# Transposing the attention's exponentials directly in front of P's first part, and splitting the attention one and a half slots sooner

## The chip, the cores and the metric

The kernel runs on one core of one Trainium2 chip. The metric is the device time of one execution in microseconds (us), the median of the runs of one version. Engines are called as the profile calls them: PE (matrix multiplication) with PEld (its weight loads), DVE (vector), ACT (scalar, activations), POOL, and SP, whose queue issues most transfers.

## What is computed

An attention between 512 tokens and 32 states per head (8 batches, 8 heads, 64 wide) feeds two gated blocks of matrix products:

```python
def _attn_ref(x, state):                 # x: 8,8,512,64   state: 8,8,32,64
    scores = scale * np.matmul(x, state.transpose(0, 1, 3, 2))
    ...
    xread = np.matmul(a, state)          # a: softmax over the 32 states
    ...
    sread = np.matmul(a2, x)             # a2: softmax over the 512 tokens
    return np.concatenate([xread, sread], axis=2)
...
    h = (x @ w1) * (x @ w2) @ w3         # 4352 rows, 512 -> 1024 -> 1024
    x = h @ w_out                        # -> 512
    h = x @ w_in                         # -> 2048
    return (h * np.clip(h + 3, 0, 6) / 6) @ w_out2
```

## The kernel before

All matrix products of full size are done three times, with high and low halves of split operands (`mm3`, L87 to L90): a value is rounded to its high half on ACT (`rnd`, L71), and the rest is taken on DVE (`rest`, L79).

The program has two phases. The change lies in the first, which goes over the 8 batches b. The states are first multiplied into w1 and w2, and this product is called P. A batch has 8 **slots** m = 0 to 7, each with 128 columns of the hidden width. A slot does this (function `slot`):

- PE makes two products `ps_ab` of P (split: `ph`, `pl`) with the normalized attention (split: `Ah`, `Al`), 12 matmuls each of 128x512;
- ACT copies the first to `asb`, DVE multiplies the second with it to `ab` (L630), ACT rounds `ab` to `abh`, DVE takes the rest `abl`;
- PE does the 12 matmuls that multiply the `abh`, `abl` of two slots before with the folded w3 (`x2_mm`, output `x`), in two halves of 6 with a place between them that the code calls `mid`.

Slot 4 does no second part; its two `ps_ab` and those of slot 5 follow each other.

The attention of batch b+1 is prepared during the slots of batch b by the generator `attention`, one step at a time: `step()` is called once a slot right behind the multiplication (`before`) and once at `mid`. Its operations here are

- `e2_t`: eight PE transposes of the exponentials e2 into two PSUM banks `ps_e` (L250); `e2_out`: two ACT copies of these to `e2t` (L255);
- `turn`: two DVE transposes of the normalized attention into `aT` (L311); then `Ah` (ACT, L71) and `Al` (DVE, L79): this is the splitting;
- `sread`: 32 small matmuls with `e2t` as weights, into `ps_r` (L262), and `sread_div`, which scales them on ACT (L270); `sread_out` stores them.

P is made in visits: two in slot 0 and slot 6 at `mid` and a pair at the end of slot 3. The visit of slot 6 is P's first part of the next batch (`p_mm`, 16 small matmuls into two banks `ps_p`, L446; then `p_split`: `ph` on ACT, `pl` on DVE).

A third stream, `stream2`, unpacks, combines and splits the weights of the second phase during the first batches, up to batch 5, in pieces called by `pump`, also twice a slot. Its ACT pieces here are `sh` (the high half, into a single buffer from which SP's queue stores it to DRAM) and `hd`; its DVE pieces are `sl`, `cm`, `ts`, `hd` and `w`.

The order of the instructions on every engine is that in which the code is written (`manual_schedule`); each engine runs its own in order and waits on semaphores. The products `ps_ab`, `ps_e`, `ps_p` and `ps_r` share four PSUM banks (tag `b`); a new one takes a bank that an older one has left, and its first matmul waits until that one was read out. By the built program, the second bank of P in slot 6 is the one that slot 5's second product left, which is read by slot 5's `ab`.

Of the kernel before, what the change touches and what calls it, by code (L numbers as in the profile page):

```python
# [7 lines left out]
F32 = mybir.dt.float32  # L8
F32R = mybir.dt.float32r
# [10 lines left out]
def attn_moe_kernel(tc, xt_d, xn_d, st_d, wa, wb, wc, wi, wo, out):  # L20
# [19 lines left out]
    B, H, S, D, NS = 8, 8, 512, 64, 32  # L40
# [12 lines left out]
    def open_pool(key, **kw):  # L53
        es[key] = ExitStack()
        return es[key].enter_context(tc.tile_pool(name=key, **kw))
# [10 lines left out]
    def bank(name):  # L66
        return psum.tile([128, 512], F32, tag="b", name=name, bufs=4)
# [9 lines left out]
    def rest(out_, in_, hi, eng):  # L77
        e = nc.gpsimd if eng == "P" else nc.vector
        e.tensor_tensor(out=out_, in0=in_, in1=hi.bitcast(F32), op=ALU.subtract)  # L79
# [30 lines left out]
    att = open_pool("att", bufs=1, side=right)  # L110
# [105 lines left out]
    def attention(b, fine=False):  # L216
# [6 lines left out]
        e2 = att.tile([128, 2, 512], F32, tag="e2", name="e2")  # L223
# [21 lines left out]
        def e2_t(u):  # L245
            ps = bank("ps_e")
            for k in range(2):
                for g in range(2):
                    t = 2 * u + k
                    nc.tensor.transpose(ps[:, (2 * k + g) * 128:(2 * k + g + 1) * 128],  # L250
                                        e2[:, g, t * 128:(t + 1) * 128], ident)
            return ps

        def e2_out(u, ps):
            nc.scalar.copy(out=e2t[:, 2 * u:2 * u + 2].rearrange("p t g k -> p (t g k)"), in_=ps)  # L255

        def sread():
            ps = bank("ps_r")
            for g in range(2):
                for t in range(T):  # L260
                    for c in range(4):
                        nc.tensor.matmul(ps[NS * c:NS * c + NS, 64 * g:64 * g + 64], e2t[:, t, g, NS * c:NS * c + NS],  # L262
                                         xn[:, t, 128 * c + 64 * g:128 * c + 64 * g + 64], start=(t == 0),
                                         stop=(t == T - 1))
            return ps
# [8 lines left out]
        def sread_out(ps, sr):  # L274
            if b == B - 1:
                ps = ps[:, 128:256]
                nc.tensor.transpose(ps, sr, ident)
                nc.scalar.copy(out=xs_r[:, :, b * NS:], in_=ps.rearrange("p (c n) -> p c n", c=4))
                t = att.tile([128, T, DM], F32R, tag="xn", name="xs_hl").rearrange("p (i a) f -> p i (a f)", i=2)
                xs_hl.extend(t[:, i].rearrange("p (k f) -> p k f", k=KD) for i in range(2))  # L280
                rnd(xs_hl[0], xs_r, "A")
                rest(xs_hl[1], xs_r, xs_hl[0], "V")
                return
            xs = att.tile([128, 4, NS], F32, tag="xs", name="xs")
            nc.vector.transpose(out=xs.rearrange("p j n -> p (j n)"), in_=sr)
            for c in range(4):
                nc.sync.dma_start(out=xsd[:, c, b * NS:(b + 1) * NS].rearrange("(j i) n -> i j n", i=32),
                                  in_=xs[32 * c:32 * c + 32])
# [27 lines left out]
        if fine:  # L316
            ps = scores()
# [8 lines left out]
        else:  # L326
            ps = scores()
# [17 lines left out]
        if b == 1:  # L345
            ps = e2_t(0)
            yield
            e2_out(0, ps)
            sum_n()
            yield  # L350
            e2_out(1, e2_t(1))
            div_n()
            yield
            ps = sread()
            aT = att.tile([128, 2, 512], F32, tag="e2", name="aT")
            turn(aT)
            yield
            sr = sread_div(ps)
        elif fine:
            ps = e2_t(0)  # L360
            yield
            e2_out(0, ps)
            sum_n()
            yield
            ps = e2_t(1)
            yield
            e2_out(1, ps)
            div_n()
            yield
            ps = sread()  # L370
            aT = att.tile([128, 2, 512], F32, tag="e2", name="aT")
            turn(aT)
            yield
            sr = sread_div(ps)
        else:
            sum_n()
            yield
            div_n()
            for _ in range(4):
                yield  # L380
            ps = [e2_t(u) for u in range(2)]
            for u in range(2):
                e2_out(u, ps[u])
            yield
            aT = att.tile([128, 2, 512], F32, tag="e2", name="aT")
            turn(aT)
            yield
        pool = late if b % 2 else mid
        A_h = pool.tile([128, 2, 512], F32R, tag="Ah", name="Ah")
        A_l = pool.tile([128, 2, 512], F32R, tag="Al", name="Al")  # L390
        A_t[b] = (A_h, A_l)
        rnd(A_h, aT, "A")
        yield
        if not fine:
            ps = sread()
            sr = sread_div(ps)
            yield
            if b == B - 1:
                sread_out(ps, sr)
                yield  # L400
        rest(A_l, aT, A_h, "V")
        if b == B - 1:
            return
        if not fine:
            yield
        sread_out(ps, sr)

# [2 lines left out]
    def step():  # L410
        if live:
            try:
                next(live[0])
            except StopIteration:
                live.pop(0)
# [5 lines left out]
    with tc.manual_schedule():  # L421
# [15 lines left out]
        def p_mm(v):  # L437
            b, mm = divmod(v, 4)
            ps = p_ps[v] = [bank("ps_p") for c in range(2)]

            o = 256 * (mm % 2)
            for c in range(4):
                w = w12[mm // 2, c].rearrange("p (i f) -> p i f", i=2)[:, :, o:o + 256]
                for r in range(2):
                    h = slice(64 * r, 64 * r + 64)
                    nc.tensor.matmul(ps[r][NS * c:NS * c + NS], st_t[b][h, c, :], w[h], start=True, stop=True)  # L446
# [229 lines left out]
        def ws_split(u, to):  # L676
            h, l = to
            rnd(h, w12[u // 4, u % 4], "A")
            rest(l, w12[u // 4, u % 4], h, "V")
            wsp[u // 4, u % 4] = h, l  # L680
# [190 lines left out]
        for b in range(B):  # L871
            if 0 < b < B - 1:
                live.append(attention(b + 1))
            if b == B - 2:
                for _ in second:
                    pass
                close_pool("cvs")
                wsq = open_pool("wsq", bufs=1, side=right, reuse_waits="tile")
            if b == B - 1:
                xs_h, xs_l = xs_hl  # L880
                s_block()
                close_pool("wsq")
                close_pool("att")
                xb = open_pool("xb", bufs=1, side=right, reuse_waits="tile")
                first = combos(0)
                next(first)
            A = A_t.pop(b)
            for m in range(0 if b else 4, M1):
                if m == (6 if b else 5) and b + 2 < B:
                    load_x(b + 2)  # L890

                def pump(i):
                    nonlocal room
                    room += (ROOM if b else ROOM0)[m][i]
                    while room > 0:
                        room -= next(second, 99)

                def before():
                    step()
                    if b == 0 and m == 7:  # L900
                        step()
                    pump(0)

                visits = {0: (1,), 3: (2, 3), 6: (4,)} if b else {4: (3,), 6: (4,)}
                visits = [4 * b + k for k in visits.get(m, ()) if 4 * b + k < 4 * B]

                def mid_():
                    if len(visits) == 1:
                        p_mm(visits[0])
                        p_split(visits[0])  # L910
                    step()
                    pump(1)
                slot(b, m, A, before, mid_, visits if len(visits) > 1 else ())
                if b == B - 2 and m >= 2:
                    if m == 2:
                        xs_r = wsq.tile([128, KD, SR], F32, name="xs_r")
                        n = (B - 1) * NS
                        nc.sync.dma_start(out=xs_r[:, :, :n], in_=xsd[:, :, :n])
                    ws_split(m - 2, [wsq.tile([128, 1024], F32R, tag=f"ws{hl}", name=f"ws{hl}", bufs=6) for hl in "hl"])
                if b == B - 1:  # L920
                    for _ in range((3, 4, 4, 4, 1, 2, 2, 1)[m]):
                        next(first, None)
            drain_att()
# [485 lines left out]
```

## Time and profile before

| | us |
|---|---|
| median of 3 runs | 1174.78 |
| lowest and highest run | 1174.6, 1174.9 |
| the profiled execution's own time | 1175.26 |
| its span, first to last instruction | 1173.5 |

PE is busy for 1166.4 us of the span, DVE for 861.1, ACT for 547.3. The first phase's batches 1 to 6, in which the change lies, run from 115 to 422 us. A PE row's start is a time at which the matmul began; its end is modelled, so the distance of two starts is the better measure of what something costs.

### The profile page before, as it was taken

The numbers are of one execution on the slowest core, as the hardware profiler recorded it, in microseconds if no ns is written. First come the engines' busy times: TensorE is split into PE (matmuls) and PEld (weight loads), VectorE is DVE, ScalarE is ACT, GpSimd is POOL, SyncE is SP. The second block draws the span as 40 slices with busy tenths as digits, with TensorE's granted clock in tenths as the row PEclk, the third lists the DMA queues.
The fourth block names the chain that finished last, engine by engine and source line by source line (L and its number), as shares of the span: only waits on it lengthen the run. The fifth ranks groups of instructions, "written<-read, shape, count | busy, mean of one in ns | idle before, by whom it ended". The sixth has DMA issues, their size and how long they took to land.

```text
span 1173.5 us, 16465 instructions
## 1 busy us (share of the span) xinstructions
PE 1166.4 (99%) x6335; PEld 930.3 (79%) x6335; DVE 861.1 (73%) x1238; ACT 547.3 (47%) x808; POOL 45.3 (4%) x59
## 2 busy tenths in 40 slices
PE   9999999999999999999999999999999999999998
PEld 6467777777777789788888888888888888888887
DVE  7999988989895652646678766778667786557483
ACT  3545655556554552534455344453444543335341
POOL 0000000000000000000110000010000100001100
PEclk9999999999999999999999999999999999999999
DMA  9853767868665101357889877998788976436973
GB/s 358 319 194 142 237 202 241 274 216 282 220 229 171 52 37 37 117 181 222 265 252 304 259 235 228 275 301 246 230 275 240 300 239 204 148 131 183 246 230 72
DMA packets 119263, 252.10 MB, mean 215 GB/s; under 512 B 45584, under 2 KB 63504, under 8 KB 112784
## 3 DMA queue, kind: packets, MB, share of 16 engines
q1 hardware_dynamic: 109888, 221.94, 54.9%
q0 software_dynamic: 7632, 27.79, 11.8%
q10 hardware_dynamic: 1664, 1.31, 0.3%
q8 instruction: 50, 0.82, 0.3%
q14 instruction: 29, 0.24, 0.1%
HBM read 181.86 MB, written 47.64 MB: 196 GB/s over the span
## 4 chain that ended last, share of the span: by engine, by line
PE 97%; DMA 1%; DVE 1%; ACT 0%; SPq 0%; issue 0%; ACTq 0%; DVEq 0%
PE ps L1072 26%; PE ps_d L1235 26%; PE x L88 6%; PE x L89 5%; PE x L90 5%; PE ps_ab L88 5%; PE ps_w L508 5%; PE ps_ab L89 5%; PE ps_ab L90 5%; PE ps_p L446 3%; PE ps_hs L1072 2%; PE ps_so L1248 2%; DMA swih<-sh 1%; PE ps_sb L89 1%; PE ps_sb L90 1%; PE ps_sb L88 1%
## 5 line engine op out<-in xcount | busy, mean ns | idle before, releaser
L1072 PE MATMUL ps<-xc,wah 128*128 128x512 f32 x512 | 157.9, 390 | 0.0
L79 DVE TENSOR_TENSOR hlj<-g,hlj 128x1024 fp32r<-128x1024 f32 x85 | 103.5, 1217 | 35.3 <-ACT hlj L71 33.8
L1002 ACT ACTIVATE rl<-c,half 128x512 f32<-128x512 f32 x96 | 69.5, 724 | 116.6 <-DVE c L972 67.8
L1072 PE MATMUL ps<-xc,wbh 128*128 128x512 f32 x384 | 118.3, 390 | 0.0
L1235 PE MATMUL ps_d<-hlj,wah 128*128 128x512 f32 x384 | 118.3, 389 | 0.0
L71 ACT ACTIVATE hlj<-g 128x1024 fp32r<-128x1024 f32 x85 | 89.5, 1057 | 49.9 <-PE ps_d L1235 44.8
L88 PE MATMUL x<-abh,w3ph 128*128 128x512 f32 (+1 forms) x288 | 112.1, 389 | 0.0
L1072 PEld LDWEIGHTS ps<-xc,wah 128*128 128x128 f32 x512 | 95.7, 188 | 19.4
L89 PE MATMUL x<-abl,w3ph 128*128 128x512 f32 (+1 forms) x288 | 109.2, 379 | 0.0
L90 PE MATMUL x<-abh,w3pl 128*128 128x512 f32 (+1 forms) x288 | 108.8, 378 | 0.0
L88 PE MATMUL ps_ab<-Ah,ph 128*128 128x512 f32 x256 | 100.6, 393 | 0.2 <-DVE pl L79 0.2
L89 PE MATMUL ps_ab<-Al,ph 128*128 128x512 f32 x256 | 99.8, 390 | 0.0
L90 PE MATMUL ps_ab<-Ah,pl 128*128 128x512 f32 x256 | 99.8, 390 | 0.0
L1072 PE MATMUL ps<-xc,wal 128*128 128x512 f32 x256 | 99.7, 389 | 0.0
L1235 PE MATMUL ps_d<-hlj,wbh 128*128 128x512 f32 x292 | 90.1, 390 | 0.0
L1235 PEld LDWEIGHTS ps_d<-hlj,wah 128*128 128x128 f32 x384 | 72.1, 188 | 14.9
L1072 PEld LDWEIGHTS ps<-xc,wbh 128*128 128x128 f32 x384 | 72.0, 188 | 14.8
L71 ACT ACTIVATE abh<-ab 128x512 fp32r<-128x512 f32 (+1 forms) x72 | 43.7, 607 | 84.4 <-DVE ab L630 84.3
L1072 PE MATMUL ps<-xc,wbl 128*128 128x512 f32 x192 | 74.8, 390 | 0.0
L1235 PE MATMUL ps_d<-hlj,wal 128*128 128x512 f32 x192 | 74.8, 389 | 0.0
L88 PEld LDWEIGHTS x<-abh,w3ph 128*128 128x128 f32 x288 | 54.2, 188 | 22.4 <-issue 11.7
L1005 DVE SCALAR_TENSOR_TENSOR g<-rl,c 128x512 f32<-128x512 f32 x96 | 65.8, 685 | 8.1 <-ACT rl L1002 8.1
(185 smaller groups left out, 2279.5 us busy)
## 6 DMA issues: line engine op xcount, KB each, us to landing
g<-g POOLq DMA_DIRECT2D x41, 512.0 KB, 6.9
wah<-swih SPq DMA_DIRECT2D x32, 512.0 KB, 4.2
wal<-swil SPq DMA_DIRECT2D x32, 512.0 KB, 5.3
wah<-swoh SPq DMA_DIRECT2D x32, 512.0 KB, 4.4
wal<-swol SPq DMA_DIRECT2D x32, 512.0 KB, 5.4
wbh<-swih SPq DMA_DIRECT2D x32, 384.0 KB, 4.8
wbl<-swil SPq DMA_DIRECT2D x32, 384.0 KB, 5.4
wbh<-swoh SPq DMA_DIRECT2D x32, 384.0 KB, 5.3
```

Of the source, the lines that this page charges most:

```text
L71: nc.scalar.activation(out=out_, in_=in_, func=AF.Copy)
L79: e.tensor_tensor(out=out_, in0=in_, in1=hi.bitcast(F32), op=ALU.subtract)
L88: nc.tensor.matmul(ps, lh, rh, start=first, stop=False)
L89: nc.tensor.matmul(ps, lh, rl, start=False, stop=False)
L90: nc.tensor.matmul(ps, ll, rh, start=False, stop=last)
L446: nc.tensor.matmul(ps[r][NS * c:NS * c + NS], st_t[b][h, c, :], w[h], start=True, stop=True)
L508: nc.tensor.matmul(w3_ps[m], t[:, o:o + 128], wout[k], start=k == 0, stop=k == M1 - 1)
L1002: nc.scalar.activation(out=rl, in_=c, func=AF.Relu, bias=half, scale=sign / 6.0)
L1005: nc.vector.scalar_tensor_tensor(out=o, in0=rl[:, a:a + n], scalar=1.0, in1=c[:, a:a + n], op0=ALU.min, op1=ALU.mult)
L1072: nc.tensor.matmul(ps, u[:, k, :], v[:, k, :], start=first and k == 0 and i == 0, stop=k == 1 and i == 2, skip_group_check=True)
L1235: nc.tensor.matmul(ps[:, f], a, x[:, k, f], start=begin, stop=n == NG - 1 and z == 2, skip_group_check=True)
L1248: nc.tensor.matmul(d["s"][q][:, 256 * e:256 * e + 256], a, x[:, n, :], start=i == 0 and n == 0 and z == 0, stop=i > 1 and n == NG - 1 and ...
```

## The change

For batches 2 to 7 (made during batches 1 to 6), `e2_t` and `e2_out` leave slot 5 and go to `mid` of slot 6, directly in front of P's visit, by an additional `step()`; `sread` still follows P. `turn`, `Ah` and `Al`, which stood behind `e2_t`, move up: `turn` to slot 5 behind the multiplication, `Ah` to `mid` of slot 5, `Al` to slot 6 behind the multiplication (it was in slot 7). `aT` gets a buffer of its own instead of that of e2. That takes 4 KB a partition, so one pair of split weights of the last batch moves into the buffers `aT` and `xtl`, which are free by then.

```diff
@@ -378,11 +378,7 @@
             div_n()
             for _ in range(4):
                 yield
-            ps = [e2_t(u) for u in range(2)]
-            for u in range(2):
-                e2_out(u, ps[u])
-            yield
-            aT = att.tile([128, 2, 512], F32, tag="e2", name="aT")
+            aT = att.tile([128, 2, 512], F32, tag="aT", name="aT")
             turn(aT)
             yield
         pool = late if b % 2 else mid
@@ -391,17 +387,15 @@
         A_t[b] = (A_h, A_l)
         rnd(A_h, aT, "A")
         yield
+        rest(A_l, aT, A_h, "V")
         if not fine:
+            yield
+            ps = [e2_t(u) for u in range(2)]
+            for u in range(2):
+                e2_out(u, ps[u])
+            yield
             ps = sread()
             sr = sread_div(ps)
-            yield
-            if b == B - 1:
-                sread_out(ps, sr)
-                yield
-        rest(A_l, aT, A_h, "V")
-        if b == B - 1:
-            return
-        if not fine:
             yield
         sread_out(ps, sr)
 
@@ -906,6 +900,8 @@
 
                 def mid_():
                     if len(visits) == 1:
+                        if m == 6 and 0 < b < B - 1:
+                            step()
                         p_mm(visits[0])
                         p_split(visits[0])
                     step()
@@ -916,7 +912,11 @@
...
-                    ws_split(m - 2, [wsq.tile([128, 1024], F32R, tag=f"ws{hl}", name=f"ws{hl}", bufs=6) for hl in "hl"])
+                    if m < 7:
+                        to = [wsq.tile([128, 1024], F32R, tag=f"ws{hl}", name=f"ws{hl}", bufs=5) for hl in "hl"]
+                    else:
+                        to = [att.tile([128, 1024], F32R, tag=g, name="ws5") for g in ("aT", "xtl")]
+                    ws_split(m - 2, to)
```

PE at `mid` of slot 6 in batch 2, before (x is the accumulator of the folded w3's products; `waits` names the engine or queue whose semaphore is waited for):

```order
L90 MATMUL x_1_1764<-abh,w3pl_402 128x512
L446 MATMUL ps_p<-big_419,br_1436 32x512 [waits Activation_49]
L446 MATMUL ps_p<-big_419,br_1436 32x512 [waits DVE_49]
L446 MATMUL ps_p<-big_446,br_1436 32x512 x2
L446 MATMUL ps_p<-big_507,br_1436 32x512 x2
L446 MATMUL ps_p<-big_528,br_1436 32x512 x2
L262 MATMUL ps_r<-xn,e2t 32x64 [waits DMAHW6_49,Activation_49]
L262 MATMUL ps_r<-xn,e2t 32x64 x31
```

The same place now (lines behind L380 have moved up by 6, so P is L440):

```order
L90 MATMUL x_1_1764<-abh,w3pl_402 128x512
L250 MATMUL ps_e<-ident,e_1615 128x128 [waits Activation_49]
L250 MATMUL ps_e<-ident,e_1615 128x128 x3
L250 MATMUL ps_e<-ident,e_1615 128x128 [waits DVE_49]
L250 MATMUL ps_e<-ident,e_1615 128x128 x3
L440 MATMUL ps_p<-big_419,br_1427 32x512 [waits Activation_49]
L440 MATMUL ps_p<-big_419,br_1427 32x512 [waits DVE_49]
L440 MATMUL ps_p<-big_446,br_1427 32x512 x2
L440 MATMUL ps_p<-big_507,br_1427 32x512 x2
L440 MATMUL ps_p<-big_528,br_1427 32x512 x2
L262 MATMUL ps_r<-xn,e2t 32x64 [waits DMAHW6_49,Activation_49]
L262 MATMUL ps_r<-xn,e2t 32x64 x7
```

The transposes stand between the half of x and P. P's banks are others now: by the built program, its second matmul waits for the multiplication `ab` of slot 6 itself, no longer for that of slot 5; and sread waits for ACT a second time ahead of its ninth matmul, which is the first that reads the second copy of `e2t`.

ACT in slot 6 of batch 3, before:

```order
L628 COPY asb<-ps_ab_2505 128x512 [waits PE_49,Activation_49]
L71 ACTIVATE Ah<-aT 128x1024 [waits DVE_49]
L71 ACTIVATE sh<-w 128x768 [waits DMAHW6_49,DMAHW5_49,Activation_49]
L71 ACTIVATE sh<-cm 128x1024 [waits DVE_49]
L71 ACTIVATE abh<-ab 128x512 [waits DVE_49]
L71 ACTIVATE ph<-ps_p 128x512 [waits PE_49] x2
L270 ACTIVATE sr<-ps_r,mr 128x64 [waits PE_49]
```

The same now, with `Ah` of slot 5's `mid` ahead:

```order
L71 ACTIVATE Ah<-aT 128x1024 [waits DVE_49]
L622 COPY asb<-ps_ab_2496 128x512 [waits PE_49,Activation_49]
L71 ACTIVATE sh<-w 128x768 [waits DMAHW5_49,DMAHW6_49,DVE_49,Activation_49]
L71 ACTIVATE sh<-cm 128x1024 [waits DVE_49]
L71 ACTIVATE abh<-ab 128x512 [waits DVE_49]
L255 COPY e2t<-ps_e 128x512 [waits PE_49] x2
L71 ACTIVATE ph<-ps_p 128x512 [waits PE_49] x2
L270 ACTIVATE sr<-ps_r,mr 128x64 [waits PE_49]
```

The two copies `e2t` stand behind `abh` of slot 6, which stands behind the two pieces `sh` of the weight stream, and in front of `ph`; `Ah` has moved ahead of `asb`.

DVE from slot 5 to slot 6 of batch 2, before (the first row's `ab` is slot 5's, the second `ab` is slot 6's):

```order
L630 TENSOR_TENSOR ab<-ps_ab_1918,asb 128x512 [waits PE_49,Activation_49]
L578 TENSOR_TENSOR w<-w,hd 128x1024 [waits DVE_49]
L79 TENSOR_TENSOR abl<-ab,abh 128x512 [waits Activation_49]
L311 STREAM_TRANSPOSE aT<-sN 128x512 [waits PE_49]
L311 STREAM_TRANSPOSE aT<-sN 128x512
L79 TENSOR_TENSOR sl<-w,sh 128x768 [waits DMAHW1_49,DMAHW0_49]
L79 TENSOR_TENSOR sl<-cm,sh 128x1024
L630 TENSOR_TENSOR ab<-ps_ab_1978,asb 128x512 [waits PE_49,Activation_49]
L596 TENSOR_TENSOR cm<-w 128x256 [waits DVE_49]
L597 TENSOR_TENSOR cm<-w 128x256
L598 TENSOR_TENSOR cm<-cm,w 128x256 [waits DVE_49]
L599 TENSOR_TENSOR cm<-w,cm 128x256 [waits DVE_49]
```

The same now:

```order
L624 TENSOR_TENSOR ab<-ps_ab_1918,asb 128x512 [waits PE_49,Activation_49]
L311 STREAM_TRANSPOSE aT<-sN 128x512 x2
L572 TENSOR_TENSOR w<-w,hd 128x1024 [waits DVE_49]
L79 TENSOR_TENSOR abl<-ab,abh 128x512 [waits Activation_49]
L79 TENSOR_TENSOR sl<-w,sh 128x768 [waits DMAHW1_49,DMAHW0_49]
L79 TENSOR_TENSOR sl<-cm,sh 128x1024
L624 TENSOR_TENSOR ab<-ps_ab_1969,asb 128x512 [waits PE_49,Activation_49]
L79 TENSOR_TENSOR Al<-aT,Ah 128x1024 [waits DVE_49]
L590 TENSOR_TENSOR cm<-w 128x256 [waits DVE_49]
L591 TENSOR_TENSOR cm<-w 128x256
L592 TENSOR_TENSOR cm<-cm,w 128x256 [waits DVE_49]
L593 TENSOR_TENSOR cm<-w,cm 128x256 [waits DVE_49]
```

`turn` (L311) has moved ahead of slot 5's `abl`, but still stands ahead of slot 6's `ab`; `Al` stands between slot 6's `ab` and its `abl`.

## Rows read from the trace of the kernel before

**Rows 1.** The page: busy time of each engine, and the chain that ended last.

```profile
PE 1166.4 (99%) x6335; PEld 930.3 (79%) x6335; DVE 861.1 (73%) x1238; ACT 547.3 (47%) x808; POOL 45.3 (4%) x59
...
PE 97%; DMA 1%; DVE 1%; ACT 0%; SPq 0%; issue 0%; ACTq 0%; DVEq 0%
```

**Rows 2.** Timeline of PE, batch 2, slots 5 and 6: start, duration in us, instruction.

```profile
204.15 0.39 PE L90 MATMUL ps_ab<-Ah,pl 128*128 128x512 f32 x1
204.38 1.03 PE L250 MATMUL ps_e<-ident,e 128*128 128x128 f32 x8
205.17 0.48 PE L88 MATMUL x<-abh,w3ph 128*128 128x512 f32 x1
205.48 0.40 PE L89 MATMUL x<-abl,w3ph 128*128 128x512 f32 x1
...
211.84 0.39 PE L90 MATMUL x<-abh,w3pl 128*128 128x512 f32 x1
212.16 1.09 PE L446 MATMUL ps_p<-big,br 64*32 64x512 f32 x16
213.18 1.10 PE L262 MATMUL ps_r<-xn,e2t 128*32 128x64 f32 x64
214.21 0.50 PE L88 MATMUL x<-abh,w3ph 128*128 128x512 f32 x1
```

**Rows 3.** Timeline of DVE: `ab` of slot 6 in batches 2, 3, 5; slot 5's `abl` in batch 5.

```profile
212.06 0.68 DVE L630 TENSOR_TENSOR ab<-ps_ab,asb 128x512 f32<-128x512 f32 x1
...
263.01 0.68 DVE L630 TENSOR_TENSOR ab<-ps_ab,asb 128x512 f32<-128x512 f32 x1
...
361.48 0.69 DVE L79 TENSOR_TENSOR abl<-ab,abh 128x512 fp32r<-128x512 f32 x1 [1.05 <-ACT abh L71]
...
365.28 0.68 DVE L630 TENSOR_TENSOR ab<-ps_ab,asb 128x512 f32<-128x512 f32 x1
```

**Rows 4.** Timeline of ACT, batch 2: slot 5's copies `e2t`, slot 6's `abh` and `ph`.

```profile
205.54 1.07 ACT L255 COPY e2t<-ps_e 128x512 f32<-128x512 f32 x2
...
212.77 0.63 ACT L71 ACTIVATE abh<-ab 128x512 fp32r<-128x512 f32 x1 [1.51 <-DVE ab L630]
213.34 1.08 ACT L71 ACTIVATE ph<-ps_p 128x512 fp32r<-128x512 f32 x2
```

**Rows 5.** Groups by line: ACT's copies `e2t`, busy time and mean ns of one.

```profile
L255 ACT COPY e2t<-ps_e 128x512 f32<-128x512 f32 x16 | 8.8, 588 | 6.3 <-PE ps_e L250 6.3
```

**Rows 6.** sread's weight loads (L262): ns of one, min/median/max.

```profile
L262 PEld LDWEIGHTS ps_r<-xn,e2t x512: 106/110/111, 60.3 to 418.0; 128*32 128x32 f32 x171
```

**Rows 7.** Timeline of PE: slot 6 of batches 3 and 5.

```profile
263.05 1.09 PE L446 MATMUL ps_p<-big,br 64*32 64x512 f32 x16
264.06 0.54 PE L262 MATMUL ps_r<-xn,e2t 128*32 128x64 f32 x24
...
365.31 1.09 PE L446 MATMUL ps_p<-big,br 64*32 64x512 f32 x16
```

**Rows 8.** Timeline of ACT, batch 3, slot 6.

```profile
264.59 0.84 ACT L71 ACTIVATE sh<-w 128x768 fp32r<-128x768 f32 x1 [1.84 <-DMA swih<-sh]
...
266.29 0.62 ACT L71 ACTIVATE abh<-ab 128x512 fp32r<-128x512 f32 x1
266.81 1.06 ACT L71 ACTIVATE ph<-ps_p 128x512 fp32r<-128x512 f32 x2
```

**Rows 9.** Timeline of PE, batch 3, slot 7.

```profile
267.72 0.39 PE L90 MATMUL ps_ab<-Ah,pl 128*128 128x512 f32 x1
268.29 0.50 PE L88 MATMUL ps_ab<-Ah,ph 128*128 128x512 f32 x1 [0.18 <-DVE pl L79]
```

**Rows 10.** Stretches at the end: length, busy PE, PEld, DVE, ACT, POOL, granted clock, DMA share, GB/s.

```profile
1168.00:1170.00 2.00, 0.72 (x7) 0.51 (x5) 1.09 (x3) 0.00 (x0) 0.00 (x0) 1.00 0.40 80
1170.00:1171.50 1.50, 0.00 (x0) 0.00 (x0) 0.00 (x0) 0.00 (x0) 0.00 (x0) 1.00 0.90 190
1171.50:1173.50 2.00, 0.00 (x0) 0.00 (x0) 0.00 (x0) 0.00 (x0) 0.00 (x0) 0.59 0.18 40
```

## The prediction

> **What bounds the kernel now.** I read the page first: PE is busy for 99% of the span, and the chain that ended last is PE's to 97% [rows 1]. So a change can gain only what PE spends beside its large matmuls, and loses whatever makes PE wait. DVE is busy for 73% and ACT for 47% [rows 1], but that is a mean: in slots 4 to 6 of batches 1 to 4, where the weight stream runs, DVE works without a pause and is behind PE. What counts is therefore where DVE and ACT stand at the moment at which PE comes to the new place. For that I read the timelines of PE, DVE and ACT in slots 5 and 6.
>
> On PE, matmuls of 128x512 start 0.23 us apart (204.15 to 204.38, no loss on entering the transposes). The eight transposes take 0.79 (204.38 to 205.17), and the large matmul behind them needs 0.31 to the next, 0.08 more than its 0.23 [rows 2]. P is entered 0.32 after the last large matmul, 0.09 more than 0.23; sread follows 1.02 later and takes 1.03 [rows 2].
>
> **What the change can save.** The transposes themselves stay, 0.79 a batch. What goes is the return from them to large matmuls (0.08) and, if the step from transposes to P costs nothing, P's own entry (0.09). The trace has no transposes in front of P; its bounds are 0 and the 0.09 of P's entry, so the saving lies between 0.08 and 0.17 a batch, for six batches 0.5 to 1.0 us. It counts only where PE does not wait right behind, and that is where the rest of the sum comes from.
>
> **P's second matmul now waits for slot 6's own multiplication.** With the transposes in slot 6, P's second bank is the one that slot 6's `ab` reads. In batch 2, `ab` runs from 212.06 to 212.74 [rows 3]. PE would be ready for P at about its old 212.16 less the saving (the 0.87 that leaves slot 5 comes back as 0.79 here) [rows 2]. DVE's order up to this `ab` holds the same work as before: `turn` moves from behind slot 5's `abl` to ahead of it, both ahead of slot 6's `ab`, and DVE has no idle time between that slot 4's `ab` and this one, so `ab` ends no sooner. With 0.05 for the semaphore (ACT started 0.03 after this end [rows 3, 4]) P's second matmul starts at 212.79, 0.63 later than the old P. Whatever the step from transposes to P costs disappears in this wait. Behind that matmul PE's whole queue waits, since PE takes its matmuls in order.
>
> **sread now waits for copies made at the last moment.** ACT starts `abh` at 212.77 and is free at 213.34 [rows 4]. There `ph` began; now the two copies come first. The transposes are long done by then, so ACT does not wait. The pair takes 1.07 and one copy 0.59 [rows 4, 5]: they end at 213.93 and 214.41. The exponentials are sread's weights, so a load of 0.11 follows [rows 6], and with 0.05 for the semaphore the ninth matmul, the first of the second copy, can start at 214.57. Before, it started a quarter of sread's 1.03 behind 213.18, at 213.44 [rows 2]. This batch ends 1.13 us later than before, P's 0.63 included. Without load and semaphore it would be 0.97. Batches 1 and 4 read the same within 0.1, so three batches cost 3 x 1.13 = 3.4.
>
> **Batch 3 is worse.** There ACT waits 1.84 for the store of the last `sh` to DRAM before it may write the next one (264.59), does both pieces, reaches `abh` at 266.29 and is free at 266.81 [rows 8]. So far nobody minds: P's banks have until slot 7, and what is late costs PE one start distance of 0.57 in place of 0.23, that is 0.34 [rows 9]. Now the copies stand behind this `abh`: 266.81 + 1.07 + 0.16 = 268.04 for sread's ninth matmul, which before started at 264.06 + 0.26 = 264.32 [rows 7]. That is 3.72, less the old 0.34, since slot 7 moves along: 3.4. `ab` alone (263.01 to 263.69 [rows 3], P at 263.05 [rows 7]) would have cost 0.7 of it. The store is issued behind a load whose buffer DVE frees, and DVE is paced by PE, so I let this wait move along with the delays of batches 1 and 2.
>
> **Batches 5 and 6.** In batch 5 DVE idles for 1.05 before slot 5's `abl` [rows 3]; `turn` now fills it, so slot 6's `ab` ends at 365.96 - 1.05 = 364.91, before P (365.31 [rows 7]). Second copy: 364.91 + 0.03 + 0.57 + 1.07 = 366.58, ninth matmul at 366.74 against 365.31 + 1.02 + 0.26 = 366.59 before: 0.15 lost at most. In batch 6 the stream is over and only the saving remains. Together about 0.
>
> **What costs nothing.** `Al` moves ahead of slot 6's `abl` on DVE, about 1.2 us of work. Behind it wait `abl` (used two slots later, over 5 us) and `pl` of P, whose bank is wanted by slot 7's second product, 12 large matmuls (2.8 us) behind the end of sread. `ph` then ends about 0.6 to 1.1 behind the copies, so `pl` has about 2 us; if that cover went, slot 7 would wait as batch 3 did, 0.3. `Ah` moves to a gap of ACT. `sread_out`'s four small stores come half a slot sooner on SP's queue; nothing reads them before batch 6. The moved weight pair writes into buffers that sread and `Al` left over a slot before.
>
> **The clock.** A stall of this size has a second danger. PE's last matmul ends at 1168.72; the granted clock still stands at 1.00 up to 1171.50, 2.8 us behind it, and has a mean of 0.59 over the 2.00 us after that, so there it fell to its lower level [rows 10]. In batch 3 PE would stand still from the end of P (263.74 + 1.02) to about 267.5, 2.7 us: in the row the clock was still full after that much, and the sum stays. The Trainium skill, page "TensorE: Matmul & The Clock Gate", section "Why this matters for your kernels", warns of pauses between bursts of matmuls in the middle of a kernel, since they bring the clock back to its lower level; no row of this trace shows such a pause between matmuls. If it happens, PE works at 1.2 in place of 2.4 GHz for a while; taken, as an estimate, to be as long as the stall, 2.7 us, this loses 1.4 us.
>
> **The sum.** 3.4 (batches 1, 2, 4) + 3.4 (batch 3) + 0 (batches 5, 6) = 6.8. The load and the semaphore (0.16 in four batches, 0.6) may be partly hidden, since a weight load can stand ready; I take half off: 6.5. The profiled execution took 1175.26 with a span of 1173.5, 0.5 above the median; the shift is applied to the median: 1174.78 + 6.5 = **1181.3**, and a span of about 1180.0.
>
> **Rivals.**
> - *The store of batch 3 lands in time.* If ACT's wait of 1.84 [rows 8] vanishes, batch 3 costs 1.5 and the sum is 4.7: 1179.5. For it: transfers vary by some us. Against it: the order of ACT and of SP around it is unchanged. Chance 0.15.
> - *The clock falls in batch 3's stall*, as above: 1181.3 + 1.4 = 1182.7. Chance 0.12.
> - *The waits don't arise (other side).* If DVE and ACT come to slot 6 earlier than in the old trace, the transposes go straight over into P and only the saving of 0.5 to 1.0 remains: 1174.0. It decides at 1.1 us: `ab` of slot 6 must end that much sooner in batches 1 to 4, as it does in batch 5, where `turn` fills a hole. Against it: DVE has no such hole in batches 1 to 4. With half of it, the time is about 1177. Chance 0.10.
> - *The forecast*: chance 0.63.
>
> **Numbers.** A measurement of this kernel can tell about 0.2%, 2.3 us, from no change. The forecast and its two neighbours are slower (0.90); of the third, most lies within 2.3 us. So faster 0.02, same 0.09, slower 0.89. The range takes in the store that lands in time with the smaller prices of the waits (1178.0) and the clock's fall with a longer low stretch (1184.0).
>
> **What would show it.** In the changed kernel's trace: P's row in slot 6 of batches 1 to 4 broken after its first start, with a wait for DVE's `ab`; sread's row starting later than 1.02 behind P, with a wait for ACT's `e2t`, 2 to 3 us in batch 3; neither in batches 5 and 6; transposes to P without a large matmul between; the second phase as long as before. The granted clock of the stretch behind batch 3's stall tells whether it fell. The prediction is wrong if `ab` of slot 6 ends more than 0.5 us sooner against P, or if ACT passes `sh` of batch 3 without waiting.

## The result, and the profile after

| | before | changed |
|---|---|---|
| median of 5 runs, us | 1174.60 | 1182.47 |
| lowest and highest | 1174.46, 1174.90 | 1180.89, 1184.36 |
| span of the profiled execution | 1173.5 | 1180.7 |

The changed kernel is slower by 0.66%, little but clear of the noise: the ratio of the times is 1.0066, with a 95% interval of [1.0055, 1.0077]. 1181.3 was forecast, and the range 1178.0 to 1184.0 holds it. The executions of the changed kernel spread over 3.5 us, those of before over 0.4; the clock, below, goes along with most of it.

All of it lies in batches 1 to 4. The second phase, the last 663.5 us of either span, has the same PE time, 658.72 before and 658.74 after. From P's visit in slot 0 of one batch to that of the next, PE's timelines give 1.08, 1.02, 4.29 and 1.03 us more than before for batches 1 to 4, and 0.01 less for batch 5. First batch 2, in the timeline of PE of the changed kernel (start, duration, instruction), then batch 3 and batch 5 of the same view:

```profile
212.09 0.39 PE L90 MATMUL x<-abh,w3pl 128*128 128x512 f32 x1
212.32 1.03 PE L250 MATMUL ps_e<-ident,e 128*128 128x128 f32 x8
213.29 1.73 PE L440 MATMUL ps_p<-big,br 64*32 64x512 f32 x16
215.07 1.36 PE L262 MATMUL ps_r<-xn,e2t 128*32 128x64 f32 x64
216.36 0.50 PE L88 MATMUL x<-abh,w3ph 128*128 128x512 f32 x1
216.70 0.39 PE L89 MATMUL x<-abl,w3ph 128*128 128x512 f32 x1
...
263.99 0.39 PE L90 MATMUL x<-abh,w3pl 128*128 128x512 f32 x1
264.22 1.03 PE L250 MATMUL ps_e<-ident,e 128*128 128x128 f32 x8
265.19 1.80 PE L440 MATMUL ps_p<-big,br 64*32 64x512 f32 x16
269.25 2.00 PE L262 MATMUL ps_r<-xn,e2t 128*32 128x64 f32 x64 [2.26 <-ACT e2t L255]
271.18 0.80 PE L88 MATMUL x<-abh,w3ph 128*128 128x512 f32 x1
271.77 0.63 PE L89 MATMUL x<-abl,w3ph 128*128 128x512 f32 x1
...
371.58 0.39 PE L90 MATMUL x<-abh,w3pl 128*128 128x512 f32 x1
371.81 1.03 PE L250 MATMUL ps_e<-ident,e 128*128 128x128 f32 x8
372.78 1.09 PE L440 MATMUL ps_p<-big,br 64*32 64x512 f32 x16
373.80 1.10 PE L262 MATMUL ps_r<-xn,e2t 128*32 128x64 f32 x64
374.83 0.50 PE L88 MATMUL x<-abh,w3ph 128*128 128x512 f32 x1
375.16 0.39 PE L89 MATMUL x<-abl,w3ph 128*128 128x512 f32 x1
```

Batch 5 is the measure of what the three groups take when nothing is waited for: from the last large matmul to the next 3.25 (371.58 to 374.83). Batch 2 takes 4.27 for the same, 1.02 more: P's row is 1.73 long in place of 1.09, and sread comes 1.78 behind P's start in place of 1.02. Batch 3 takes 7.19, 3.94 more, and behind it the first two large matmuls start 0.59 apart (271.18 to 271.77), in place of 0.33 in batch 5 (374.83 to 375.16). P's longer row is the sign of a wait inside the group. PE's own list of waits doesn't show it, since a matmul's modelled end covers it; the reader has to look at the distance of the starts, or at the waits of the weight loads (PEld), which in batch 2 name `ab` for P (0.5) and `e2t` for sread (1.2 in two waits).

Who is late in batch 2 shows on DVE and ACT of the same kernel, in their timelines:

```profile
213.19 0.68 DVE L624 TENSOR_TENSOR ab<-ps_ab,asb 128x512 f32<-128x512 f32 x1
213.79 1.22 DVE L79 TENSOR_TENSOR Al<-aT,Ah 128x1024 fp32r<-128x1024 f32 x1
```

```profile
213.91 0.63 ACT L71 ACTIVATE abh<-ab 128x512 fp32r<-128x512 f32 x1 [2.78 <-DVE ab L624]
214.45 1.05 ACT L255 COPY e2t<-ps_e 128x512 f32<-128x512 f32 x2
```

`ab` ends at 213.87, 0.58 behind P's start; ACT passes it on as `abh`, and the copies run from 214.45 to 215.50, while sread starts at 215.07, just behind the first of them.

In batch 3, ACT before that:

```profile
266.42 0.84 ACT L71 ACTIVATE sh<-w 128x768 fp32r<-128x768 f32 x1 [3.65 <-DMA swih<-sh]
267.17 1.04 ACT L71 ACTIVATE sh<-cm 128x1024 fp32r<-128x1024 f32 x1
268.11 0.61 ACT L71 ACTIVATE abh<-ab 128x512 fp32r<-128x512 f32 x1
268.63 1.05 ACT L255 COPY e2t<-ps_e 128x512 f32<-128x512 f32 x2
269.58 1.09 ACT L71 ACTIVATE ph<-ps_p 128x512 fp32r<-128x512 f32 x2
```

It is the chain of [rows 8], with the copies behind it, and with a wait for the store that became longer (3.65 for 1.84): ACT is free for `sh` at the same time as before (262.77 for 262.75), because `Ah` no longer stands between `asb` and it, but the store lands 1.83 later. The stretches around it, with the same columns as [rows 10] (PE busy is the second number, the granted clock the third from the right):

```profile
266.00:268.00 2.00, 0.99 (x15) 0.08 (x14) 1.97 (x4) 1.58 (x2) 0.00 (x0) 1.00 1.10 402
268.00:269.00 1.00, 0.00 (x0) 0.00 (x0) 1.00 (x2) 1.00 (x3) 0.00 (x0) 1.00 0.90 330
269.00:270.00 1.00, 0.69 (x28) 0.53 (x32) 0.51 (x1) 1.00 (x3) 0.00 (x0) 0.79 1.07 360
270.00:273.00 3.00, 3.00 (x52) 2.50 (x45) 2.42 (x3) 2.25 (x5) 0.00 (x0) 0.50 0.96 287
273.00:274.00 1.00, 1.00 (x6) 0.79 (x5) 0.00 (x0) 0.00 (x0) 0.00 (x0) 1.00 0.67 189
```

PE stands still for 2.26, and the clock, full during the pause, is at its lower level (0.50, that is 1.2 GHz) from about 269.6 to 273.0, after sread has begun. Of the five timed executions, the profiled one (1182.47) shows this fall in its trace, with a mean clock of 0.999; three more show 0.996 to 0.998, less than any of the 36 executions of the kernel before that were timed beside the experiments (0.999 or 1.000), and take 1182.47 to 1184.36; one shows 1.000 and takes 1180.89. So the clock fell in four of the five; for three of them only the mean clock says so.

### The profile page after: what moved, and what is told of

The parts are those of the page before. It is cut to its first block, busy times and chain, and to the rows that moved or that the text cites. A ratio compares the mean times of both kernels' runs of the same rounds, so it can differ in the third digit from the quotient of the medians.

```text
span 1180.7 us, 16464 instructions
## 1 busy us (share of the span) xinstructions
PE 1171.9 (99%) x6335; PEld 933.8 (79%) x6335; DVE 862.0 (73%) x1238; ACT 547.5 (46%) x808; POOL 45.4 (4%) x59
## 4 chain that ended last, share of the span: by engine, by line
PE 95%; DVE 3%; ACT 1%; DMA 1%; issue 0%; SPq 0%; POOL 0%; DVEq 0%; POOLq 0%; ACTq 0%
PE ps L1072 26%; PE ps_d L1235 26%; PE x L88 5%; PE x L89 5%; PE x L90 5%; PE ps_w L502 5%; PE ps_ab L88 4%; PE ps_ab L89 4%; PE ps_ab L90 4%; PE ps_p L440 2%; PE ps_hs L1072 2%; PE ps_so L1248 2%; PE ps_i L421 1%; PE ps_r L262 1%; DMA swih<-sh 1%; PE ps_sb L89 1%
## 5 line engine op out<-in xcount | busy, mean ns | idle before, releaser
L624 DVE TENSOR_TENSOR ab<-ps_ab,asb 128x512 f32<-128x512 f32 x64 | 44.0, 688 | 42.6 <-PE ps_ab L90 41.0
```

The costliest lines, as they stand in the source:

```text
L624: nc.vector.tensor_tensor(out=ab[:, :n], in0=psb[:, :n], in1=a[:, :n], op=ALU.mult)
```

## The experiments

The theory: P waits for slot 6's own multiplication and sread for the copies of `e2t`, because both now stand directly behind the transposes; batch 3 adds the store that ACT waits for, and the clock that falls behind PE's pause. The first rival: the earlier splitting is to blame, with `Al` in front of `abl` and `pl` on DVE.

**Each half alone.** Run `split_only` leaves the transposes in slot 5 and keeps the earlier splitting:

```diff
+            ps = [e2_t(u) for u in range(2)]
+            for u in range(2):
+                e2_out(u, ps[u])
             aT = att.tile([128, 2, 512], F32, tag="aT", name="aT")
...
-            ps = [e2_t(u) for u in range(2)]
-            for u in range(2):
-                e2_out(u, ps[u])
-            yield
             ps = sread()
...
-                        if m == 6 and 0 < b < B - 1:
-                            step()
```

> Half of the change alone: aT has its own buffer and turn, Ah and Al are made as early as in the changed kernel, but the transposes and their copies stay in slot 5. Theory (PE waits for slot 6's multiplication and for the copies of e2t, because the transposes stand directly in front of P and sread): none of the waits arises, the time is that of the kernel before, 1174.6 within 0.5. Rival (the earlier splitting puts Al in front of abl and pl on DVE and delays what P and slot 7 need): most of the 7.9 us is here, 1179 to 1182.

Run `transposes_only` leaves the splitting where it was, and moves the transposes:

```diff
-            for _ in range(4):
+            for _ in range(5):
                 yield
             aT = att.tile([128, 2, 512], F32, tag="aT", name="aT")
...
-        rest(A_l, aT, A_h, "V")
         if not fine:
-            yield
             ps = [e2_t(u) for u in range(2)]
...
+            yield
+            if b == B - 1:
+                sread_out(ps, sr)
+                yield
+        rest(A_l, aT, A_h, "V")
```

> The other half alone: transposes and copies directly in front of P's visit of slot 6, with turn, Ah and Al at their old places (aT keeps its own buffer). Theory: the waits of the changed kernel in batches 1 to 4 are all here, and since turn no longer fills DVE's 1.05 us of idle time in slot 5 of batch 5, that batch waits as well, about 1.1 us: 1182.5 + 1.1, so 1182 to 1185. Rival (splitting): 1174 to 1175.

Measured: 1174.71 for the splitting alone, ratio 1.0001 [0.9992, 1.0010]; 1183.47 for the transposes alone, ratio 1.0073 [1.0060, 1.0086]. The rival falls. The median of the transposes alone is 1.0 above that of the whole change; the intervals of the two overlap, so the times alone don't tell them apart, but batch 5 in PE's timeline of `transposes_only` does: its rows have the shape of batch 2 in the changed kernel:

```profile
371.52 1.03 PE L250 MATMUL ps_e<-ident,e 128*128 128x128 f32 x8
372.49 1.80 PE L446 MATMUL ps_p<-big,br 64*32 64x512 f32 x16
374.34 1.36 PE L262 MATMUL ps_r<-xn,e2t 128*32 128x64 f32 x64
```

So the half of the change that moves the splitting forward spares batch 5 about this 1 us: with `turn` in DVE's idle time, `ab` is ready there.

**DVE's lateness.** Run `stream_later` changes only the table that deals out the weight stream:

```diff
-    ROOM = ((3, 4), (4, 1), (5, 3), (1, 0), (4, 5), (4, 4), (5, 4), (4, 4))
+    ROOM = ((3, 4), (4, 1), (5, 3), (1, 0), (4, 5), (4, 0), (5, 4), (4, 8))
```

> The changed kernel, with the weight stream's pieces of slot 5's second call moved to slot 7's second call (the table ROOM alone). DVE then has two pieces less to do between slot 4 and slot 6's multiplication. Theory (DVE is late at slot 6 because of the stream, and ACT with it): the waits for ab, for e2t and the pause in batch 3 go, the granted clock stays at 1.00, and the time is that of the kernel before within 1 us, 1174 to 1175.5. Rival (standing directly in front of P costs by itself, through the step between kinds of matmuls or the order on ACT): the time stays at 1180 to 1183.

Measured: 1175.89, ratio to before 1.0009 [1.0000, 1.0018]: 6.6 of the 7.9 us are back, though it came out 0.4 above the stretch that was expected. The three groups now look alike in all six batches; batch 3 in PE's, ACT's and DVE's timelines:

```profile
261.89 0.39 PE L90 MATMUL x<-abh,w3pl 128*128 128x512 f32 x1
262.12 1.03 PE L250 MATMUL ps_e<-ident,e 128*128 128x128 f32 x8
263.09 1.09 PE L440 MATMUL ps_p<-big,br 64*32 64x512 f32 x16
264.11 1.10 PE L262 MATMUL ps_r<-xn,e2t 128*32 128x64 f32 x64
265.14 0.50 PE L88 MATMUL x<-abh,w3ph 128*128 128x512 f32 x1
```

```profile
262.32 0.63 ACT L71 ACTIVATE abh<-ab 128x512 fp32r<-128x512 f32 x1 [1.65 <-DVE ab L624]
262.86 1.05 ACT L255 COPY e2t<-ps_e 128x512 f32<-128x512 f32 x2
```

```profile
261.60 0.68 DVE L624 TENSOR_TENSOR ab<-ps_ab,asb 128x512 f32<-128x512 f32 x1
```

`ab` ends at 262.28, before P, the copies end at 263.91, before sread, and the three groups take 3.25 again. Standing directly in front of P therefore costs nothing by itself. The run takes work from ACT as well as from DVE; that DVE is the late one in batch 2 shows in the changed kernel, where ACT had waited 2.78 for `ab`. Of the 1.2 us that are left, 1.0 lies in batch 5, where in slot 0 small matmuls of the next attention (`ps_s`) take 1.81 for 1.06 and their weight loads wait for `asb` (0.9) and `ab` (0.6). That the moved pieces of the stream cause this is likely, but no run tests it.

**The store.** Run `store_other_queue` issues the stores of the high halves on POOL's queue, in the changed kernel; `store_other_queue_before` does the same to the kernel before:

```diff
-                    nc.sync.dma_start(out=to[:, at:at + n, :],
+                    (nc.sync if hl else nc.gpsimd).dma_start(out=to[:, at:at + n, :],
```

> The changed kernel, with the stores of the weight stream's high halves sh issued on POOL's queue, where nothing stands ahead of them, and not on SP's behind a load. Theory (batch 3 costs so much because ACT waits for the store of sh, and the copies and sread behind it): in batch 3 ACT no longer waits or waits under 0.3, the pause falls from about 3 us to under 1, the clock stays at 1.00: 1174.7 + 4.3 = 1179.0; batches 1, 2 and 4 as in the changed kernel. Rival (batch 3 is late for another reason): 1181 to 1183.

> The kernel before with the same move of these stores to POOL's queue, as the control. Theory: PE never waits for them there but for the 0.34 of slot 7 in batch 3, so 1174.3 to 1175. Rival (the queue itself changes the time): more than 1 us either way.

Measured: 1179.43, ratio 1.0038 [1.0025, 1.0051], and for the control 1174.59, ratio 0.9998 [0.9989, 1.0007]. ACT in batch 3 of `store_other_queue`:

```profile
263.59 0.85 ACT L71 ACTIVATE sh<-w 128x768 fp32r<-128x768 f32 x1 [0.49 <-DVE sl L79]
265.61 1.06 ACT L71 ACTIVATE sh<-cm 128x1024 fp32r<-128x1024 f32 x1 [1.17 <-DVE cm L593]
266.57 0.61 ACT L71 ACTIVATE abh<-ab 128x512 fp32r<-128x512 f32 x1
```

The wait for the store is gone, what remains is DVE; PE's one recorded wait for `e2t` falls from 2.26 to 0.4, and the clock stays at 1.00. The store was worth about 3 us, clock included.

**The order on ACT.** Run `copies_first` takes the step of the transposes ahead of `abh`, at the same place of PE's order:

```diff
             def mid():
+                if early:
+                    step()
                 hi = ab_hi(ab, 512)
...
-                        if m == 6 and 0 < b < B - 1:
-                            step()
                         p_mm(visits[0])
```

> The changed kernel, with the step that makes the transposes and their copies taken at the same place of PE's order but written ahead of slot 6's abh, so that on ACT the copies of e2t no longer stand behind abh. Theory: sread's wait in batches 1, 2 and 4 (0.5 each) goes, P's wait for ab stays (0.3 to 0.6 each), and batch 3 keeps its pause, since both stand behind the sh that waits for the store: about 3.6 us above the kernel before, 1178.3, and up to 1.5 more if the clock falls. Rival (the copies alone are late, all of it hangs on abh): 1175 to 1176.

Measured: 1178.81, ratio 1.0035 [1.0022, 1.0047]. Batches 1 and 3 in PE's timeline:

```profile
161.29 1.39 PE L440 MATMUL ps_p<-big,br 64*32 64x512 f32 x16
162.62 1.10 PE L262 MATMUL ps_r<-xn,e2t 128*32 128x64 f32 x64
...
263.70 1.80 PE L440 MATMUL ps_p<-big,br 64*32 64x512 f32 x16
267.48 1.36 PE L262 MATMUL ps_r<-xn,e2t 128*32 128x64 f32 x64 [1.97 <-ACT e2t L255]
```

In batch 1 sread's wait is gone and 0.3 of P's remains, but this is not a test of the order alone: by the built program, P's second matmul in batches 1 and 2 now takes a bank that a copy of `e2t` left, and no longer waits for `ab`. In batch 4 the banks are those of the changed kernel; there P waits as before (0.64), sread not at all, and the three groups take 3.89 for 4.28. In batch 3 the pause remains, as expected of a wait that stands ahead of both. The clock stayed at 1.00 in this profiled execution, after a pause of 1.97; another of its five executions has a mean clock of 0.998 and took 1180.33, 1.5 above the median.

**sread apart from the copies.** Run `sread_later`:

```diff
                         p_split(visits[0])
-                    step()
+                    if m != 6 or not 0 < b < B - 1:
+                        step()
                     pump(1)
```

> The changed kernel, with sread half a slot later (behind the multiplication of slot 7) and its store at the middle of slot 7. Theory: sread itself no longer waits, P's wait for ab stays (0.6 in each of batches 1 to 4, 2.4), but the late copies of e2t still hold a PSUM bank: the next product to take it, slot 7's, waits in batch 3 for about 1.1, the return from small to large matmuls is paid once more a batch (0.2, 1.2 in all) and batch 7's small operands come half a slot later, about 1: 1180 to 1182 with the granted clock at 1.00. Rival (only sread's closeness to the copies costs): 1177 to 1178.

Measured: 1180.91, ratio 1.0051 [1.0038, 1.0063]. Two rows of the list of PE's waits in this kernel (total, times, longest):

```profile
PE ps_sb L89 <- DVE xs_hl L79: 0.9, 1, 0.9
PE ps_ab L88 <- ACT e2t L255: 0.8, 1, 0.8
```

The wait for the copies came back one product later, in batch 3, through the PSUM bank that they read; the first row is a wait in batch 7 for its small operands, which come later now, as was expected. Batch 3 is 1.49 longer than before in place of 4.29, and the clock stayed at 1.00 there. P's wait for `ab` stayed: batches 1, 2 and 4 are longer by 0.86 to 0.91. Giving sread more time helps in part only, as long as DVE and ACT are late.

**The clock.** Run `p_four_times` gives PE something to do during the pause:

```diff
-                        p_mm(visits[0])
+                        p_mm(visits[0], 4 if (b, m) == (3, 6) else 1)
...
-            for c in range(4):
+            for c in [*range(4)] * times:
```

> The changed kernel, with the 8 products of P's visit in slot 6 of batch 3 alone made four times over (the same values into the same banks, 2.6 us more work for PE), so that PE works through most of the pause in front of sread. Theory (the pause lets the clock fall, and the low clock behind it costs about 1.7 us): sread starts no later, the granted clock stays at 1.00 there, and the time falls to about 1180.8 though PE does more. Rival (the clock's fall is only seen, the pause is the whole cost): 1182.5 as the changed kernel, or up to 2.6 more if the pause was not what PE waited out.

Measured: 1180.97 (1180.92 to 1181.77), ratio to before 1.0055 [1.0042, 1.0067]: 1.5 below the changed kernel's median, with 2.6 us more of matmuls, and equal to the one execution of the changed kernel whose clock did not fall (1180.89). PE's timeline and stretches:

```profile
265.10 4.38 PE L440 MATMUL ps_p<-big,br 64*32 64x512 f32 x64
269.41 1.31 PE L262 MATMUL ps_r<-xn,e2t 128*32 128x64 f32 x64
270.65 0.50 PE L88 MATMUL x<-abh,w3ph 128*128 128x512 f32 x1
270.99 0.39 PE L89 MATMUL x<-abl,w3ph 128*128 128x512 f32 x1
```

```profile
268.00:270.00 2.00, 1.99 (x58) 0.72 (x45) 1.62 (x2) 2.00 (x5) 0.00 (x0) 1.00 0.94 360
270.00:272.00 2.00, 2.00 (x54) 1.69 (x47) 1.68 (x3) 1.99 (x5) 0.00 (x0) 1.00 1.04 258
```

sread starts at about the same time (269.41 for 269.25), the clock is 1.00, and sread takes 1.24 (269.41 to 270.65) for 1.93. From slot 0 to slot 0, batch 3 is 3.00 longer than before in place of 4.29; batches 1, 2 and 4 are as in the changed kernel within 0.02.

## Why the prediction was right, step by step

- **The saving.** Forecast 0.08 to 0.17 a batch, taken as about 0 in the sum. Measured about 0: 3.25 for the three groups in batch 5. Before, the transposes took 1.02 from the last large matmul to the next and P with sread 2.37 [rows 2]; less one start distance of 0.23, with the 0.08 of the return, that is 3.24. The step from transposes to P costs what the return and P's entry had cost: it is 0.18 (0.97 from the first transpose to P, for 0.79 to a large matmul), outside the bounds of 0 and 0.09 that were taken for it. The sum didn't suffer, since it counted no saving.
- **P's wait and sread's wait.** Forecast 1.13 together in each of batches 1, 2 and 4; measured 1.08, 1.02 and 1.03, of which P's part in batch 2 is 0.64 (1.73 less 1.09) for 0.63. `stream_later` shows the cause, DVE's lateness at slot 6, by taking it away; batch 4 of `copies_first` shows that sread's part hangs on ACT's order.
- **Batch 3.** Forecast 3.4, as for a pause without a fall of the clock. With the clock held up by `p_four_times`, sread started within 0.2 of where it did, batch 3 was 3.00 longer than before, and the kernel was 6.28 above before (1180.97 against 1174.69 in that comparison): the forecast sum was 6.5. That the wait for the store would move along with the delays of batches 1 and 2 was right: SP issued the store at 258.05, 2.16 later than before, and ACT's wait ended 1.83 later (266.42 against 264.59 [rows 8]).
- **The clock.** This was a rival with a chance of 0.12, at 1.4 and 1182.7, and it happened in four of five executions: 1182.47. That is the step that was weighed wrongly. The forecast's own case, a clock that stays up, came in one of five, at 1180.89; the range holds the median because it was drawn to take in this rival. That 1181.3 came as near as 1.2 is in part luck: batch 3's pause cost 0.4 less than forecast, and the clock's fall, which the sum left out, 1.3 to 1.5 more. The argument against it was that in [rows 10] the clock was still full 2.8 us behind PE's last matmul, so a pause of 2.7 would pass. In the changed kernel it stood still for 2.26 (in that trace) and fell all the same, so the row did not bear the conclusion. The page "TensorE: Matmul & The Clock Gate" of the Trainium skill, in its section "Why this matters for your kernels", warns of such pauses between matmuls, and the trace agrees: 1.00 in the pause, 0.50 behind it. The size was right: between the changed kernel and `p_four_times` it is 1.5 in the medians and 1.3 in batch 3 of the two traces.
- **Batches 5 and 6.** Forecast 0; batch 5's three groups show no wait. `transposes_only` shows that this is owed to `turn`'s earlier place.
- **What was to cost nothing** (`Al` ahead of `abl`, the earlier stores of `sread_out`, the moved weight pair) cost nothing: `split_only` has all three, and is at 1174.71.

No run here beats the kernel before by more than can be told: the lowest is the control with the stores on the other queue, 0.9998.

## What to carry to other kernels

An operation that is put directly in front of its consumer gives up the slack that hid its evacuation: before moving it, look at where the evacuating engine stands at the new place, not at its mean busy share, and at which buffer the neighbours will now take. When a wait stands in an engine's queue harmlessly, everything that is later placed behind it inherits it, as the copies here inherited ACT's wait for a store. And a pause of PE is not paid once: it can take the clock with it.

## What the runs showed that was not expected

- From transposes to P, PE needs 0.97 from the first transpose to P's first matmul (371.81 to 372.78), against 0.79 to a large matmul [rows 2]: grouping these small matmuls of different shapes saved nothing.
- The clock's fall is not certain. In the profiled executions it fell to 0.50 behind a pause of 2.26 in the changed kernel and of 2.07 in `transposes_only`, and stayed at 1.00 behind one of 1.97 in `copies_first`. Executions of one kernel differ in it too: one of five of the changed kernel and one of five of `transposes_only` (1182.46, the others from 1183.33) have a mean clock of 1.000. Why the fall comes in one execution and not in another no run shows.
- A change of order on one engine can change which PSUM bank a product takes, and with it whom the product waits for: `copies_first` moved an operation on ACT, and in two batches P stopped waiting for DVE.
- The late copies held PE by two different ways, as sread's weights and, with sread moved off, as readers of a PSUM bank (0.8 in `sread_later`).
